# Early slots with the weights' scale alone, three late slots in a row turned by TensorE, and the loop count read after the last scatter

## The chip, the cores and the metric

The kernel runs on one core of a Trainium2 chip. The metric is the device time of one execution in microseconds (us). Three runs of the kernel before gave a median of 835.51 us (831.27 to 840.33).

## The reference

Three stages follow one another; the change touches only the last. B=4, 8 heads, 544 positions of width 64, so 2176 tokens of width 512.

```python
x = attention(q_l, k_l, v_l, q_g, k_g, v_g)      # local window of 32 and 32 global positions; 2176 x 512
h = x @ w_in;  x = (h * sigmoid(h)) @ w_out      # 512 -> 2048 -> 512
logits = x @ w_gate                              # 8 experts
e_idx = np.argmax(logits, axis=1)
gate_w = softmax(logits)[token, e_idx]
eom = 1.0 / (1.0 + np.exp(-(x @ w_output_gate)))
for e in range(8):
    mask = e_idx == e
    h = np.maximum(x[mask] @ w1[e], 0.0)         # w1[e]: 512 x 1024
    ye = h @ w2[e]                               # w2[e]: 1024 x 512
    out[mask] = gate_w[mask, None] * eom[mask, e, None] * ye
```

## The kernel before

**Stages.** Attention takes the first part of the span, the dense layers (L688, L735) follow, and their output is written row by row to `x2d` in DRAM. Each token's expert is found on the way. The expert stage fills the end, from about 530 us on.

**Slots.** The tokens of one expert are gathered into slots of 128 rows. Slots n = 0 to 7 are the early ones, one for each expert; they take tokens of the first 15 of 17 token blocks, so that their rows can be gathered before the last blocks are done. Slots n = 8 to 20 are the late ones (k = n-8 runs from 0 to 12); which expert each one has is known only after the routing. Ten further slots run only if the number of slots asks for them, inside a `tc.If` at the end. Its condition is read from the table `eidx` into a register of every engine (L1560); with these inputs it isn't met.

**Chunks.** The hidden width of 1024 is worked in 4 chunks of 256. A chunk has an h phase (`mm_h`: `hp` = slot's rows by w1, L1317 and L1320, or L1325 in another shape; then relu, a split in two f16 parts `hb` on ACT and DVE, and a DMA transpose of `hb` that SP issues, L1344) and a y phase (`mm_y`: six matmuls `yp`, L1354). The first chunk's `yp` is written out of PSUM by ACT with a factor for each row (L1362), the later chunks' by DVE, which multiplies and adds to what is there (L1364). After the last chunk POOL scatters the slot's rows to `out` (L1366). Two PSUM pools of two buffers each hold `yp`, so TensorE can be up to four slots ahead of ACT.

**The factor.** It is gate_w x eom (`cof`, one for each token) times the scale by which the expert's weights were made f16 (`gi`, one for each expert and chunk). `coefs(c)` makes their product for all slots of chunk c. For the early slots of the first chunk the product `cce` is made ahead of that by `early_coefs()`: 15 small matmuls `pce` (L1143) and some DVE operations.

**Weights.** SP loads the weights of the next chunk piece by piece (`ws`), ACT takes a maximum (L228), and ACT and DVE convert them (L961, L962) into single buffers, in place of the chunk that TensorE has just left.

**Routing.** `last()` makes, from the last two token blocks, the rows of the late slots: TensorE `pm` gives `idg` (which rows to gather), `early_coefs()` follows, then `pt` (L1196) gives `ids` (which rows to scatter to), DVE makes `eidx` and `ohs` (experts of late slots, L1140), and `pcf` (L1217) gives `cof`. `early()` sets the h phase of early slots 2 to 7 and the y phase of early slots 0 to 5 around it. `experts()` (L1244) loads the late slots' expert numbers into TensorE's registers, 13 of them.

**Late rows.** POOL gathers each late slot's rows from `x2d`. Those with k in `TURN` are turned by TensorE (8 transposes `xt` a slot, L1291; ACT or DVE copies the result out of PSUM); the others are turned by a DMA transpose that SP issues (L1260) once the gather has landed.

**Order.** The code is handed to a list scheduler, which sets the order on each engine; `high_priority` and `issue_after` bend it. An instruction waits at the head of its engine's queue, and everything behind it waits too.

Of the kernel before, what the change touches and what calls it, by code (L numbers as in the profile page):

```python
# [26 lines left out]
NE = 8  # L27
# [20 lines left out]
NS = 1  # L48
# [5 lines left out]
TURN = (1, 3, 5, 7, 9, 11)  # L54
# [53 lines left out]
def tile_kernel(ctx: ExitStack, tc, csa, csr, q0, q, qn, qg, k0, k, va, vc, w_in, w_out, wg, w1, w2, out, dbg=None):  # L108
# [876 lines left out]
    cce = const.tile([128, NEARLY], F32, name="cce")  # L985
    bnd = const.tile([128, 1, NE], F32, name="bnd")

    def route(rt, rps):
# [3 lines left out]
        def bc(x, shape):  # L992
            return x.to_broadcast(shape)
# [143 lines left out]
        def early_coefs():  # L1137
            SR = [128, 15, NEARLY]
            for c in range(3):
                DVE.tensor_tensor(Rce[:, :, c], RE, bc(cp[:, c, 0:15], SR), ALU.mult)  # L1140
            pc = rps.tile([128, 3, NEARLY], F32, tag="av", name="pce")
            for i in range(15):
                PE.matmul(pc.rearrange("p c n -> p (c n)"), A[:, i], Rce[:, i].rearrange("p c n -> p (c n)"),  # L1143
                          start=(i == 0), stop=(i == 14))
            v = T([128, 1, NEARLY], "ve")
            DVE.tensor_copy(v[:, 0], pc[:, 2])
            DVE.tensor_tensor(v[:, 0], v[:, 0], pc[:, 1], ALU.add)
            DVE.tensor_tensor(v[:, 0], v[:, 0], pc[:, 0], ALU.add)
            g = T([128, 1, NE], "ge")
            DVE.tensor_tensor(g[:, 0], i12[:, 0:NE], i12[:, NE:2 * NE], ALU.mult)  # L1150
            DVE.tensor_scalar(g, g, 2.0 ** 19, None, ALU.mult)
            DVE.tensor_tensor(cce, v[:, 0], g[:, 0], ALU.mult)

        def last():
# [34 lines left out]
            with tc.issue_after(key_i[0].ins):  # L1189
                early_coefs()  # L1190
# [39 lines left out]
    class Moe:  # L1230
        def __init__(self, slots, ne):
            self.slots, self.ne, self.ns = slots, ne, len(slots)
            self.ev, self.x, self.hT, self.ys, self.hb, self.cc = {}, {}, {}, {}, {}, {}
# [63 lines left out]
        def coefs(self, c):  # L1297
            g = cc_p.tile([128, 1, NE], F32, tag="gi", name="gi")
            DVE.tensor_tensor(g[:, 0], i12[:, 0:NE], i12[:, NE:2 * NE], ALU.mult)
            DVE.tensor_scalar(g, g, 2.0 ** 19, None, ALU.mult)  # L1300
            t = lg.rearrange("p i e -> p (i e)")[:, 0:ND * NE].rearrange("p (n e) -> p n e", e=NE)
# [4 lines left out]
            for k in range(NS):  # L1306
                r = slice(k, ST, NS)
                DVE.tensor_tensor(cc[:, r], cof[:, r], g[:, 0], ALU.mult)
# [37 lines left out]
        def mm_y(self, c, n):  # L1346
# [9 lines left out]
            if c == 0:  # L1356
# [4 lines left out]
                cc = self.cc[0][:, s:s + 1] if self.late else cce[:, n:n + 1]  # L1361
# [9 lines left out]
        def early(self, ny, i0, i1):  # L1371
            with tc.issue_after(i0.ins):
                for n in range(2, self.ne):
                    self.mm_h(n)
# [241 lines left out]
```

## Time and profile before

| | |
|---|---|
| median of three runs | 835.51 us |
| the profiled execution's own time | 835.75 us |
| its span in the trace | 834.0 us |
| PE busy | 759.4 us (91%) |
| PEld busy | 527.4 us (63%) |
| DVE busy | 600.4 us (72%) |
| ACT busy | 517.7 us (62%) |
| POOL busy | 56.8 us (7%) |

PE is TensorE's matmul, PEld its weight load (which runs beside matmuls), DVE is VectorE, ACT is ScalarE, POOL is GpSimd, SP is SyncE. Times in the rows are us from the span's start unless marked ns. An idle time in square brackets stands ahead of the instruction, with the engine, tile and line that ended it. [...]

### The profile page before, as it was taken

The numbers are of one execution on the slowest core, as the hardware profiler recorded it, in microseconds if no ns is written. First come the engines' busy times: TensorE is split into PE (matmuls) and PEld (weight loads), VectorE is DVE, ScalarE is ACT, GpSimd is POOL, SyncE is SP. The second block draws the span as 40 slices with busy tenths as digits, with TensorE's granted clock in tenths as the row PEclk, the third lists the DMA queues.
The fourth block names the chain that finished last, engine by engine and source line by source line (L and its number), as shares of the span: only waits on it lengthen the run. The fifth ranks groups of instructions, "written<-read, shape, count | busy, mean of one in ns | idle before, by whom it ended". The sixth has DMA issues, their size and how long they took to land.

```text
span 834.0 us, 17487 instructions
## 1 busy us (share of the span) xinstructions
PE 759.4 (91%) x6249; PEld 527.4 (63%) x6249; DVE 600.4 (72%) x1653; ACT 517.7 (62%) x1020; POOL 56.8 (7%) x110
## 2 busy tenths in 40 slices
PE   6999949899999989989999989998799798998995
PEld 5998726466776757667766656766566465565552
DVE  4799877767966878747755587749364878878863
ACT  3786667867847758646643895342379666856730
POOL 0000000000000000000000000032300000000144
PEclk9999969999999999999999999999999999999998
DMA  9962552658945475744545865075966746955583
GB/s 321 324 196 88 160 167 102 176 114 195 183 110 74 89 130 119 153 77 77 110 62 103 258 202 153 13 188 131 201 134 189 228 83 171 258 109 165 151 186 104
DMA packets 176235, 126.25 MB, mean 151 GB/s; under 512 B 155149, under 2 KB 156941, under 8 KB 172944
## 3 DMA queue, kind: packets, MB, share of 16 engines
q1 hardware_dynamic: 172784, 115.10, 56.7%
q0 software_dynamic: 3360, 9.97, 4.2%
q8 instruction: 54, 0.88, 0.4%
q14 instruction: 37, 0.30, 0.1%
HBM read 76.93 MB, written 9.96 MB: 104 GB/s over the span
## 4 chain that ended last, share of the span: by engine, by line
PE 41%; DMA 12%; DVE 7%; ACT 5%; issue 3%; SPq 1%; POOLq 0%; ACTq 0%; DVEq 0%
PE h L688 9%; PE x L735 9%; PE yp L1354 9%; PE hp L1325 6%; DMA ws<-in_w_dram 5%; DMA pT<-pb 4%; PE hp L1317 2%; PE av L538 2%; DMA wil<-hb 1%; DVE w1b L962 1%; ACT w1b L961 1%; DMA woh<-yx 1%; PE hp L1320 1%; ACT junk L228 1%; ACT w2b L961 1%
## 5 line engine op out<-in xcount | busy, mean ns | idle before, releaser
L735 PE MATMUL x<-woh,g 128*128 128x512 f16 x544 | 172.3, 379 | 3.5 <-ACT g L718 1.5
L688 PE MATMUL h<-xT,wih 128*128 128x256 f16 (+1 forms) x1152 | 160.4, 271 | 10.1 <-DMA xT<-xb 4.9
L735 PEld LDWEIGHTS <-g 128*128 128x128 f16 x816 | 76.4, 98 | 85.3 <-issue 2.7
L688 PEld LDWEIGHTS <-wih 128*128 128x128 f16 x1152 | 108.1, 100 | 34.2 <-DMA xT<-xb 5.2
L1354 PE MATMUL yp<-w2b,wil 128*128 (+1 forms) x384 | 93.7, 391 | 11.0 <-ACT w2b L961 5.3
L735 PE MATMUL x<-wol,g 128*128 128x512 f16 x272 | 103.1, 379 | 0.0
L688 PE MATMUL h<-xT,wil 128*128 128x256 f16 (+1 forms) x576 | 88.0, 272 | 0.0
L690 ACT ACTIVATE tanh<-h,th 128x512 f32<-128x512 f32 (+1 forms) x72 | 47.2, 658 | 64.0 <-PE h L688 61.4
L470 ACT ACTIVATE e<-e,mx,esc 128x192 f32<-128x192 f32 (+1 forms) x128 | 70.1, 549 | 18.5 <-DVE mx L467 15.5
L1354 PEld LDWEIGHTS <-wil 128*128 128x128 f16 x384 | 38.1, 103 | 51.4 <-DMA wil<-hb 8.4
L707 ACT ACTIVATE g<-tanh,i_out 128x512 f16<-128x512 f32 (+1 forms) x64 | 44.1, 691 | 33.3 <-DVE tanh L703 33.2
L228 ACT ACTIVATE junk<-ws 128x1024 f16<-128x1024 f32 x48 | 50.4, 1052 | 17.4 <-DMA ws<-in_w_dram 17.2
L466 DVE CUSTOM_DVE_ANT_0 e<-s,cs 128x192 f32<-128x192 f32 (+1 forms) x128 | 42.5, 367 | 23.2 <-PE s L455 10.4
L688 PEld LDWEIGHTS <-wil 128*128 128x128 f16 x576 | 54.4, 100 | 7.4 <-issue 0.5
L708 DVE SCALAR_TENSOR_TENSOR g<-tanh,i_out,g 128x512 f16<-128x512 f32 (+1 forms) x64 | 45.6, 713 | 17.0 <-ACT g L707 16.9
L703 DVE SCALAR_TENSOR_TENSOR tanh<-tanh,h 128x512 f32<-128x512 f32 (+1 forms) x64 | 41.4, 649 | 21.3 <-ACT tanh L690 21.0
L962 DVE SCALAR_TENSOR_TENSOR w1b<-ws,s,w1b 128x1024 f16<-128x1024 f32 x32 | 40.4, 1280 | 17.2 <-ACT w1b L961 17.0
L1325 PE MATMUL hp<-w1b,x 128*128 128x256 f16 x384 | 48.7, 279 | 1.2 <-ACT r L1338 1.2
L1325 PEld LDWEIGHTS <-x 128*128 128x128 f16 x384 | 38.6, 102 | 10.7 <-issue 2.1
L523 DVE SCALAR_TENSOR_TENSOR pb<-e,pb 128x384 f16<-128x384 f32 (+1 forms) x48 | 27.6, 586 | 22.9 <-ACT pb L522 22.8
L962 DVE SCALAR_TENSOR_TENSOR w2b<-ws,s,w2b 128x1024 f16<-128x1024 f32 x32 | 40.2, 1280 | 2.6 <-ACT w2b L961 2.6
L1364 DVE SCALAR_TENSOR_TENSOR yx<-yp,cc,yx 128x512 f32<-128x512 f32 x39 | 29.1, 748 | 8.9 <-PE yp L1354 8.8
(361 smaller groups left out, 1447.6 us busy)
## 6 DMA issues: line engine op xcount, KB each, us to landing
ws<-in_w_dram SPq DMA_DIRECT2D x64, 512.0 KB, 4.5
st<-in_w_out_dram SPq DMA_DIRECT2D x8, 1024.0 KB, 5.0
st<-in_w_in_dram SPq DMA_DIRECT2D x6, 1024.0 KB, 12.0
q<-in_q_dram SPq DMA_DIRECT2D x12, 512.0 KB, 4.0
x2d<-x2s SPq DMA_DIRECT2D x17, 256.0 KB, 2.7
st<-in_k_dram SPq DMA_DIRECT2D x3, 1088.0 KB, 7.0
st<-in_qn_dram SPq DMA_DIRECT2D x3, 1024.0 KB, 5.1
st<-in_va_dram SPq DMA_DIRECT2D x3, 1024.0 KB, 6.9
```

What stands on the lines that cost most here:

```text
L228: ACT.activation(junk, x, ACTF.Square, accum_out=m)
L466: DVE.tensor_tensor_reduce(dst[:, hh, 0:wt], ps[:, hh, 0:wt], mask, 1.0, -3e38, ALU.add, ALU.max, mx[:, hh:hh + 1])
L470: ACT.activation(dst[:, hh, 0:wt], dst[:, hh, 0:wt], ACTF.Exp, scale=esc[:, b:b + 1], bias=mx[:, 2 + hh:3 + hh], accum_out=sums[i][:, h:h ...
L688: PE.matmul(ps[:, f], w[:, kk, c], xj[:, l + kk, 0:n], start=(m == 0 and kk == 0), stop=(m == 2 and kk == KD - 1))
L690: pin[0] = ACT.activation(t, ps, ACTF.Tanh, scale=th[:, b:b + 1])
L703: pin[1] = DVE.scalar_tensor_tensor(t, t, 1.0, ps, ALU.add, ALU.mult)
L707: ACT.activation(hi, t, ACTF.Copy, scale=i)
L708: pin[2] = DVE.scalar_tensor_tensor(lo, t, i, hi, ALU.mult, ALU.subtract)
L735: PE.matmul(x2ps[2 * j + c], x[:, f, o], w[:, ff], start=(ff == 0 and m == 0), stop=(ff == KF - 1 and m == 2))
L962: DVE.scalar_tensor_tensor(d[:, 1], t[a], sc_, d[:, 0], ALU.mult, ALU.subtract)
L1325: PE.matmul(ps[:, 0], x[:, xl + kk], self.rows("1", n, l, kk), start=(m == 0 and kk == 0), stop=(m == 2 and kk == KD - 1))
L1354: PE.matmul(ps, h[:, hl + j], self.rows("2", n, l, j), start=(m == 0 and j == 0), stop=(m == 2 and j == KJ - 1))
```

## The change

It has three parts.

1. **Early slots carry only the weights' scale.** `early_coefs()` and `cce` go away. `scales(c)` makes `gi` alone, and `early()` calls it at its start. All early slots are written out with `gi` in every chunk, and after the last chunk ACT multiplies each of the eight by `cof` before its scatter. `coefs(c)` no longer makes products for them.
2. **TURN** goes from k = 1, 3, 5, 7, 9, 11 to k = 0, 1, 2, 4, 6, 8.
3. **The `If`'s value** is read on each engine after the last scatter (`issue_after(moe.end.ins)`) instead of where the scheduler put it.

```diff
--- before.py
+++ after.py
@@ -51,7 +51,7 @@
 ND = NSLOT - ST
 NMAIN = 21
 NEARLY = NE
-TURN = (1, 3, 5, 7, 9, 11)
+TURN = (0, 1, 2, 4, 6, 8)
 ORDER = (*range(14), 16, 14, 15)
 POS = {t: r for r, t in enumerate(ORDER)}
 URG = 2000
@@ -982,7 +982,6 @@
     eidx = const.tile([128, ND + 1], I32, name="eidx")
     ohs = const.tile([128, ND, NE], F32, name="ohs")
     idge = const.tile([128, NEARLY], I32, name="idge")
-    cce = const.tile([128, NEARLY], F32, name="cce")
     bnd = const.tile([128, 1, NE], F32, name="bnd")
 
     def route(rt, rps):
@@ -1133,23 +1132,6 @@
                 DVE.tensor_scalar(n0[:, 1], n0[:, 1], 128.0, None, ALU.max)
                 coef(14, 15)
                 static(0, 15)
-
-        def early_coefs():
-            SR = [128, 15, NEARLY]
-            for c in range(3):
-                DVE.tensor_tensor(Rce[:, :, c], RE, bc(cp[:, c, 0:15], SR), ALU.mult)
-            pc = rps.tile([128, 3, NEARLY], F32, tag="av", name="pce")
-            for i in range(15):
-                PE.matmul(pc.rearrange("p c n -> p (c n)"), A[:, i], Rce[:, i].rearrange("p c n -> p (c n)"),
-                          start=(i == 0), stop=(i == 14))
-            v = T([128, 1, NEARLY], "ve")
-            DVE.tensor_copy(v[:, 0], pc[:, 2])
-            DVE.tensor_tensor(v[:, 0], v[:, 0], pc[:, 1], ALU.add)
-            DVE.tensor_tensor(v[:, 0], v[:, 0], pc[:, 0], ALU.add)
-            g = T([128, 1, NE], "ge")
-            DVE.tensor_tensor(g[:, 0], i12[:, 0:NE], i12[:, NE:2 * NE], ALU.mult)
-            DVE.tensor_scalar(g, g, 2.0 ** 19, None, ALU.mult)
-            DVE.tensor_tensor(cce, v[:, 0], g[:, 0], ALU.mult)
 
         def last():
             with tc.high_priority(URG):
@@ -1187,7 +1169,6 @@
                         pm_i = PE.matmul(pm, A[:, i], Rc[:, i, c], start=(i == 0 and c == 0), stop=(i == NT - 1 and c == 1))
                 key_i[0] = DVE.tensor_scalar(idg, pm, -1.0, 0.0, ALU.add, ALU.max)
             with tc.issue_after(key_i[0].ins):
-                early_coefs()
                 for c in range(2):
                     DVE.tensor_tensor(Rc[:, :, c], R, bc(row[2 + c], SR), ALU.mult)
                 pm = rps.tile([128, NSLOT], F32, tag="av", name="pt")
@@ -1230,7 +1211,7 @@
     class Moe:
         def __init__(self, slots, ne):
             self.slots, self.ne, self.ns = slots, ne, len(slots)
-            self.ev, self.x, self.hT, self.ys, self.hb, self.cc = {}, {}, {}, {}, {}, {}
+            self.ev, self.x, self.hT, self.ys, self.hb, self.cc, self.gi = {}, {}, {}, {}, {}, {}, {}
             self.late, self.xg, self.pair = False, [], [None, None]
             for n, x in enumerate(slots):
                 if x < ST:
@@ -1294,18 +1275,20 @@
             else:
                 DVE.tensor_copy(x, p)
 
-        def coefs(self, c):
-            g = cc_p.tile([128, 1, NE], F32, tag="gi", name="gi")
+        def scales(self, c):
+            g = self.gi[c] = cc_p.tile([128, 1, NE], F32, tag="gi", name="gi")
             DVE.tensor_tensor(g[:, 0], i12[:, 0:NE], i12[:, NE:2 * NE], ALU.mult)
             DVE.tensor_scalar(g, g, 2.0 ** 19, None, ALU.mult)
+
+        def coefs(self, c):
+            if c not in self.gi:
+                self.scales(c)
+            g = self.gi[c]
             t = lg.rearrange("p i e -> p (i e)")[:, 0:ND * NE].rearrange("p (n e) -> p n e", e=NE)
             DVE.tensor_tensor(t, ohs, g.to_broadcast([128, ND, NE]), ALU.mult)
             cc = self.cc[c] = cc_p.tile([128, NSLOT], F32, tag="cc", name="cc")
             DVE.tensor_reduce(cc[:, ST:], t, AX.X, ALU.add)
             DVE.tensor_tensor(cc[:, ST:], cc[:, ST:], cof[:, ST:], ALU.mult)
-            for k in range(NS):
-                r = slice(k, ST, NS)
-                DVE.tensor_tensor(cc[:, r], cof[:, r], g[:, 0], ALU.mult)
 
         def mm_h(self, n):
             x = self.x[n]
@@ -1358,17 +1341,22 @@
                     self.ys[n] = ysv[:, n]
                 else:
                     self.ys[n] = self.room(n - self.ne, 1)
-                cc = self.cc[0][:, s:s + 1] if self.late else cce[:, n:n + 1]
+                cc = self.gi[0][:, 0, n:n + 1] if n < self.ne else self.cc[0][:, s:s + 1]
                 ACT.activation(self.ys[n], ps, ACTF.Copy, scale=cc)
             else:
-                DVE.scalar_tensor_tensor(self.ys[n], ps, self.cc[c][:, s:s + 1], self.ys[n], ALU.mult, ALU.add)
+                cc = self.gi[c][:, 0, n:n + 1] if n < self.ne else self.cc[c][:, s:s + 1]
+                DVE.scalar_tensor_tensor(self.ys[n], ps, cc, self.ys[n], ALU.mult, ALU.add)
+            if c == NCH - 1 and n < self.ne:
+                ACT.activation(self.ys[n], self.ys[n], ACTF.Copy, scale=cof[:, s:s + 1])
             if c == NCH - 1:
                 ins = POOL.indirect_dma_start(out=out[:, :], out_offset=bass.IndirectOffsetOnAxis(ap=ids[:, s:s + 1], axis=0),
                                               in_=self.ys[n], in_offset=None, bounds_check=NTOK - 1, oob_is_err=False)
                 tc.declare_no_dep(ins.ins, group="sc", reason="every row is written once")
                 tc.add_to_no_dep_group("sc", ins.ins)
+                self.end = ins
 
         def early(self, ny, i0, i1):
+            self.scales(0)
             with tc.issue_after(i0.ins):
                 for n in range(2, self.ne):
                     self.mm_h(n)
@@ -1557,7 +1545,9 @@
         ys_p = ctx.enter_context(tc.tile_pool(name="ys", bufs=1))
         moe.ys_p, moe.late = ys_p, True
         moe.rest(P["nye"], wq1)
-    with tc.If(nc.values_load(eidx[0:1, ND:ND + 1], min_val=0, max_val=ND) > NMAIN - ST):
+    with tc.issue_after(moe.end.ins):
+        more = nc.values_load(eidx[0:1, ND:ND + 1], min_val=0, max_val=ND)
+    with tc.If(more > NMAIN - ST):
         with ExitStack():
             moe = Moe(list(range(NMAIN, NSLOT)), 0)
             moe.ys_p, moe.late = ys_p, True
```

The rows below are each engine's program in its order, without times; `xN` stands for N alike in a row. Lines of the kernel after differ from those before: L1196 is L1177 there, L1244 L1225, L1354 L1337, L1217 L1198, L1344 L1327, L1260 L1241, L1258 L1239, L1366 L1352.

TensorE at the routing, before: the end of `pt`, then the load of the experts' numbers, ahead of early slot 2's `yp`.

```order
L1196 LDWEIGHTS A
L1196 MATMUL pt<-wil,A 128x31
L1244 TENSOR_LOAD eidx
L1244 ISA x8
L1354 LDWEIGHTS wil
L1354 MATMUL yp<-w2b,wil 128x512
```

The same place after: slot 2's six `yp` stand between `pt` and the load, and `pcf` right behind it.

```order
L1337 LDWEIGHTS wil
L1337 MATMUL yp<-w2b,wil 128x512
L1225 TENSOR_LOAD eidx
L1225 ISA x18
L1198 LDWEIGHTS A
L1198 MATMUL pcf<-wil,A 128x93
```

The load has moved behind six matmuls `yp`, and 18 register instructions instead of 8 follow it at once; 8 more stand after one slot's `yp` behind `pcf`. From `pm` on, TensorE's order was: 12 `yp`, 15 `pce`, 34 `pt`, load, 6 `yp`, 17 `pcf`, 6 `yp`, `xt` of k = 1 (16 with k = 3), one `hp` of k = 0, 6 `yp`, rest of k = 0, k = 2, 6 `yp`, `xt`, k = 1. It is now: 12 `yp`, 34 `pt`, 6 `yp`, load, 17 `pcf`, 12 `yp`, `xt` of k = 0 and 1, 6 `yp`, 6 `yp` (slot 6, formerly much later), `xt` of k = 2, `hp` of k = 0, `xt` of k = 4, `hp` of k = 1, `xt` of k = 6, `hp` of k = 2, `xt` of k = 8, k = 3, and so on. At the border between the first and the second chunk 24 `yp` now stand in a row.

SP's queue at the same time, before: the transposes of the early slots' `hb` (L1344) and of late rows (L1260, `woh` and `wol` hold them).

```order
L1344 DMA_TRANSPOSE wil<-hb 128x8x128 x3
L1260 DMA_TRANSPOSE woh<-yx 128x8x128
L1344 DMA_TRANSPOSE wil<-hb 128x8x128
L1260 DMA_TRANSPOSE woh<-yx 128x8x128
L1560 TENSOR_LOAD eidx
L1560 ISA x2
L1260 DMA_TRANSPOSE woh<-yx 128x8x128 x2
L1260 DMA_TRANSPOSE wol<-yx 128x8x128 x3
L1344 DMA_TRANSPOSE wil<-hb 128x8x128 x4
```

After:

```order
L1327 DMA_TRANSPOSE wil<-hb 128x8x128 x4
L1549 TENSOR_LOAD eidx
L1549 ISA x2
L1241 DMA_TRANSPOSE woh<-yx 128x8x128 x3
L1241 DMA_TRANSPOSE wol<-yx 128x8x128 x4
L1327 DMA_TRANSPOSE wil<-hb 128x8x128 x4
```

All four `hb` transposes stand ahead now; there are seven row transposes as before, the first of them for k = 3 instead of k = 0. SP's own read of the `If`'s value has no matmul or scatter ahead of it, only these.

POOL's end, before: the scatters of the eight early slots (`wih`), of twelve late slots, the `If` with the ten further slots inside, and one last scatter behind it.

```order
L1366 DMA out_dram<-wih,ids 2176x512 x8
L1366 DMA out_dram<-yx,ids 2176x512 x12
L1560 TENSOR_LOAD eidx
L1560 COMPARE_AND_BRANCH
L1258 DMA yx<-x2d,idg 128x1024 x10
L1366 DMA out_dram<-yx,ids 2176x512 x10
L1560 UNCONDITIONAL_BRANCH
L1560 ISA
L1560 UNCONDITIONAL_BRANCH
L1366 DMA out_dram<-yx,ids 2176x512
```

After:

```order
L1352 DMA out_dram<-wih,ids 2176x512 x8
L1352 DMA out_dram<-yx,ids 2176x512 x13
L1549 TENSOR_LOAD eidx
L1550 COMPARE_AND_BRANCH
L1239 DMA yx<-x2d,idg 128x1024 x10
L1352 DMA out_dram<-yx,ids 2176x512 x10
L1550 UNCONDITIONAL_BRANCH
L1550 ISA
L1550 UNCONDITIONAL_BRANCH
```

The thirteenth late slot's scatter has moved ahead of the read and the branch. On ACT the eight new scalings (`wih` by `cof`) stand in the last chunk among the h phase's work: four in a row ahead of one `hb`, the next three and the last one each ahead of a later `r`.

## Rows read from the trace of the kernel before

**Rows 1.** The page: the chain that ended last, share of the span by engine.
```profile
PE 41%; DMA 12%; DVE 7%; ACT 5%; issue 3%; SPq 1%; POOLq 0%; ACTq 0%; DVEq 0%
```

**Rows 2.** Table by stretch: length, busy us of PE, PEld, DVE, ACT, POOL, clock.
```profile
584.00:588.00 4.00, 3.55 (x43) 2.54 (x43) 1.62 (x7) 1.94 (x3) 3.09 (x4) 1.00 1.20 243
592.00:596.00 4.00, 1.84 (x8) 1.02 (x9) 0.04 (x1) 0.00 (x0) 0.95 (x1) 0.84 1.24 247
596.00:600.00 4.00, 4.00 (x29) 2.48 (x28) 0.69 (x1) 1.71 (x2) 0.00 (x0) 0.73 0.93 249
600.00:616.00 16.00, 16.00 (x132) 12.04 (x130) 9.53 (x24) 7.67 (x19) 0.00 (x0) 1.00 0.91 145
612.00:645.00 33.00, 33.00 (x218) 21.14 (x216) 17.57 (x44) 29.65 (x51) 0.00 (x0) 1.00 0.61 164
711.00:714.00 3.00, 3.00 (x16) 2.14 (x15) 0.95 (x4) 2.33 (x5) 0.00 (x0) 0.50 1.02 363
```

**Rows 3.** PE in order of time: start, us, line, count, [idle before <-releaser].
```profile
578.55 0.53 PE L1143 MATMUL pce<-ohs,A 128*128 128x24 bf16 x15
578.93 1.01 PE L1196 MATMUL pt<-wil,A 128*128 128x31 bf16 x34
582.58 1.47 PE L1354 MATMUL yp<-w2b,wil 128*128 128x512 f16 x6 [2.64 <-ACT wih L1362]
584.49 0.92 PE L1217 MATMUL pcf<-wil,A 128*128 128x93 bf16 x17 [0.45 <-DVE wil L1214]
...
594.15 0.93 PE L1325 MATMUL hp<-w1b,woh 128*128 x5 [3.96 <-DMA woh<-yx]
...
708.58 0.60 PE L1354 MATMUL yp<-w2b,wil 128*128 128x512 f16 x2 [2.66 <-ACT w2b L961]
```

**Rows 4.** The chain that ended last, in order of time: start, us, what.
```profile
584.29 9.73 DMA woh<-yx
...
691.61 4.06 DMA ws<-in_w_dram
...
823.88 4.69 DMA out_dram<-yx,ids
```

**Rows 5.** L1244, the experts' numbers into PE's registers: ns minimum/median/maximum.
```profile
L1244 PEldq FUSED_REGOPS  x13: 146/146/165, 581.3 to 585.3; - x13
...
L1244 PEldq TENSOR_LOAD <-eidx x1: 1319/1319/1319, 579.9 to 579.9; - x1
```

**Rows 6.** DVE in order of time around the routing.
```profile
576.26 0.67 DVE L1140 TENSOR_TENSOR ohs<-ohb,cp 128x120 bf16<-128x120 bf16 x3
...
581.13 0.15 DVE L1152 TENSOR_TENSOR cce<-ve,ge 128x8 f32<-128x8 f32 x1
...
583.72 0.71 DVE L1214 TENSOR_TENSOR wil<-wil,cp 128x527 bf16<-128x527 bf16 x1
```

**Rows 7.** Gathers of L1258 (first and last start), then landing of L1260's transposes.
```profile
L1258 POOL DMA_INDIRECT yx<-x2d,idg x7: 940/946/946, 576.6 to 592.2; - x7
...
DMA to landing us min/median/max: 3.5/8.9/12.7
```

**Rows 8.** The last scatters: POOL and DVE in order of time.
```profile
823.88 0.97 POOL L1366 DMA_INDIRECT out_dram<-yx,ids  x1 [0.33 <-DVE yx L1364]
824.15 0.75 DVE L1364 SCALAR_TENSOR_TENSOR yx<-yp,cc,yx 128x512 f32<-128x512 f32 x1 [0.54 <-PE yp L1354]
829.54 0.97 POOL L1366 DMA_INDIRECT out_dram<-yx,ids  x1 [4.68 <-DMA out_dram<-yx,ids]
```

**Rows 9.** L1366, the scatters from 780 us on: issue to landing.
```profile
DMA to landing us min/median/max: 2.5/3.3/6.0
```

**Rows 10.** L1362, ACT's eviction of a 128x512 slot, 612 to 645 us: ns.
```profile
L1362 ACT ACTIVATE yx<-yp,cc x12: 672/703/763, 623.5 to 641.2; 128x512 f32<-128x512 f32 x12
```

**Rows 11.** DVE, and ACT, in order of time in the last chunk.
```profile
792.02 0.74 DVE L1364 SCALAR_TENSOR_TENSOR wih<-yp,cc,wih 128x512 f32<-128x512 f32 x1
...
793.13 0.42 ACT L1335 ACTIVATE hb<-r 128x256 f16<-128x256 f32 x1 [4.13 <-DVE r L1334]
```

## The prediction

> **What bounds the kernel now.** I read the page's chain first: TensorE has 41% of it, more than all else together [rows 1], so a wait of TensorE is where this change can pay. The stretch table from 584 to 645 us shows where the routing costs it time: 1.84 us busy of 4.00 between 592 and 596, and the granted clock down to 0.84 and 0.73 in two stretches, then 1.00 again [rows 2]. From 612 to 645 TensorE is busy for all of the 33.00 us, with ACT at 29.65 [rows 2]: what it gains ahead of 600 is carried on, as no outside event holds it there. (The weights that it meets later are converted into buffers that it frees itself, so their loads move with it; I count on that.)
>
> TensorE in order of time names three waits: 2.64 us for ACT's eviction of an early slot, 0.45 us for DVE ahead of `pcf`, and 3.96 us for a DMA transpose ahead of slot k = 2's last matmuls [rows 3]. Sum 7.05. The transpose was issued at 584.29 and took 9.73 us [rows 4]. The clock's fall costs 4.00 x (1 - 0.84) = 0.64 and 4.00 x (1 - 0.73) = 1.08, together 1.72 us. So the routing loses 8.77 us.
>
> At the end, the last scatter is issued at 829.54, although the DVE operation that makes its rows runs from 824.15 for 0.75 us [rows 8]. It stands behind the `If`, and POOL waited 4.68 us there for the landing of the scatter before it.
>
> **A: the routing.** Removed: the 15 `pce`, 578.93 - 578.55 = 0.38 us of TensorE [rows 3], and the wait of 2.64, since ACT now needs `gi` alone, which is made long before. The wait does not simply vanish: `pcf` needs DVE's last product, and that is now the next thing that is late. Before, this product ended at 583.72 + 0.71 = 584.43 [rows 6]. Gone from DVE ahead of it are 0.67 us of `ohs` [rows 6] and eight small operations of `early_coefs` and `gi`, each like the 0.15 us of `cce` [rows 6]; they overlap, so between 0 and 1.2, and I take 0.5. `pcf` can start at 584.43 - 0.67 - 0.5 = 583.3. TensorE reaches it at 578.55 + 1.01 (`pt`) + 1.3 (six `yp`; 1.47 with the overlap [rows 3]) = 580.9. It then waits about 2.5 us. The register load must also pass: 1.32 us, and nine pairs of instructions, by the span of the 13 recorded ones (581.3 to 585.3 over 12 steps) 0.33 us at most each [rows 5], together 4.3. Started when `pt` has been handed out, near 579.5, it ends at about 583.8 and adds little; started only after the six `yp` it holds `pcf` to 585.2, a wait of 4.3. Before, its instructions ran while matmuls were still at work (581.3 to 585.3, `yp` from 582.58), so I take 2.5, bounds 2.5 to 4.3.
>
> The clock: the wait of 2.64 left it at 1.00 between 584 and 588, while a wait of 2.66 before 708.58 [rows 3] was followed by 0.50 between 711 and 714 [rows 2]. A lone wait of 2.5 can go either way: 0 or 1.72. I take 1.7.
>
> Row transposes: `TURN` now gives k = 0, 1, 2 to TensorE, and the first slot that a DMA turns is k = 3. Its gather stands one place behind that of k = 2, 1.30 us (the seven gathers shown lie at every second place of 13 from 576.6 to 592.2: 15.6 / 12) [rows 7]. If its transpose takes the same 9.73, it lands at 584.29 + 1.30 + 9.73 = 595.3. TensorE has until then: 583.3 + 0.75 (`pcf`, 0.92 with its overlap [rows 3]) + 24 `yp` (four slots of 1.3, 5.2) + the `xt` of k = 0, 1, 2, 4, 6, 8 (48 with a quarter of `yp`'s columns, so 48 x 1.3 / 6 / 4 = 2.6) + the h phases of k = 0, 1, 2 (as many columns as a `yp` slot, 3.9), in sum 595.8. That just covers it. The transposes landed 3.5 to 12.7 us after issue, 8.9 in the middle [rows 7], so a wait between 0 and the 3.96 of before; I take 0.7. The moved `xt` are the same number of instructions, 48, and their evictions lie beside the `yp`. SP's own read of the `If`'s value stands ahead of the seven transposes, at a time when SP waits for the gather anyway; I cost it at nothing, and at 1.3, as on TensorE [rows 5], if that cover is gone.
>
> A in sum: 8.77 + 0.38 - 2.5 - 1.7 - 0.7 = 4.25 us. Best, without the clock's fall and the DMA wait: 6.65. Worst: 9.15 - 4.3 - 1.72 - 3.96 = -0.8.
>
> [...]
>
> **B: the end.** Before, the last scatter was issued at 829.54; now it stands directly behind its predecessor, which was issued at 823.88 and held POOL for 0.97 us, with 0.33 between [rows 8]. It can issue at 825.2, 4.4 us sooner. The read of the `If`'s value and the branch now follow it; in the old order about 1 us lay between the predecessor's landing (823.88 + 4.69 = 828.57 [rows 4]) and 829.54, and I set that against the gain: 3.4. If the last scatter then takes the 4.69 of its predecessor [rows 4] instead of the 2.5 at the lower end [rows 9], 2.2 more are lost: 1.2. I take 2.8, near the upper bound, since the median landing is 3.3 [rows 9].
>
> **C: eight scalings on ACT**, each 0.70 us by ACT's eviction of the same shape [rows 10], 5.6 us in all. ACT sat idle for 4.13 us before `hb` at 793.13 [rows 11], which takes most of the first four. The fourth must wait for DVE's eviction that ends at 792.02 + 0.74 = 792.76 [rows 11] and ends itself at 793.46, 0.3 after the `hb` behind it could have started. I take -0.3. Without the idle time they would cost 2.8.
>
> **D and E.** `scales(0)` puts two small DVE operations far ahead of the routing, at most 0.15 us each [rows 6]: -0.2. The border between the first and the second chunk now has 24 `yp` in a row; the same work in another order, taken at nothing. If it makes weights late, each late load costs 4.06, as the one at 691.61 [rows 4].
>
> **Sum.** 4.25 + 2.8 - 0.3 - 0.2 = 6.55 us. The profiled execution took 835.75, all but the median of 835.51. 835.75 - 6.55 = 829.2 us.
>
> **The rivals.** R1, the routing runs smoothly: no fall of the clock and no late transpose, 2.4 us more, so 826.8. For it: the wait of 2.64 that cost no clock [rows 2]. Against it: the wait at `pcf` is followed by work that depends on gathers still landing. R2, DMA transposes are late again: the wait of 3.96 comes back at k = 3 instead of 0.7, 832.4. For it: the landing up to 12.7 [rows 7], and three transposes queued behind each other; against it: three slots' work now lies ahead. R3, the clock falls once more: TensorE's stretch with 48 transposes among few matmuls lowers the granted clock again, another 1.72, 830.9; the stretch 600 to 616, in which the last 16 `xt` of before lie, at 1.00 [rows 2] speaks against it. [...] R4, slower: at the border of the chunks the weights come late because 24 `yp` in a row keep the old w2 longer and no h phase hides it. It takes 6.55 of late loads (two of 4.06) to cancel the gain, and 14.9, four of them, to be slower by 1%. Nothing in the stretch 612 to 645, where TensorE is never idle, speaks for four. R5, the move of the `If` does nothing, because the end waits for the landing as before: 829.2 + 2.8 = 832.0.
>
> **How the numbers follow.** My forecast 829.2 has a chance of 0.44; R1 0.27, R2 0.15, R3 0.05, R4 0.05, R5 0.04. About 1%, 8.4 us, is what a measurement of this kernel can tell from no change, so the border lies at 827.2. R1 puts most of its chance below it, and my forecast some, as its terms are uncertain by 2 us: faster 0.38. R4's far end gives slower 0.06, and 0.56 remain within 1%. The range goes from 823.5 (R1, with the full 3.4 at the end and 2 us of the 1% scatter of the runs' median) to 834.5 (R2 with B at 1.2 and some).
>
> **What would show it.** In the changed profile: one wait of 2 to 3 us ahead of `pcf`, released by DVE; no wait for ACT's eviction; 0 to 1 us for a transpose at k = 3; a stretch near 0.75 of the clock between 584 and 600 or none; the last two scatters 1.3 us apart; and TensorE without a gap until the border of the chunks, where it would begin about 4 us earlier. Wrong would be a wait of 4 us or more at k = 3 or at `pcf`, weights later than the work, or a last scatter that lands no sooner.

## The result, and the profile after

The changed kernel took 827.37 us, the kernel before 837.32 us (medians of six runs each; three of before's six are those taken ahead of the prediction). The ratio is 0.989, with an interval of 0.985 to 0.993. In a second comparison it was 827.31 against 838.08 us, ratio 0.985 (0.979 to 0.991). The profiled execution took 825.79 us with a span of 824.0, against 835.75 and 834.0 before. The forecast was 829.2, with a gain of 6.55 us; the gain is about 10.

After `pm` the kernels run the same matmuls, apart from the 15 `pce`. So I cut each profile by counting TensorE's matmuls back from the last one and taking their start times: from the first `pm` to the 1234th before the last (the routing, into the first chunk's late slots), to the 959th (end of the first chunk), to the 534th (the border to the second chunk and beyond), to the 134th, to the 34th (the last chunk's y phase has begun), and to the span's end. Times in us; the kernels are those of the experiments below.

| kernel | first `pm` | routing | to 959 | to 534 | to 134 | to 34 | tail | span |
|---|---|---|---|---|---|---|---|---|
| before | 575.1 | 33.50 | 47.21 | 74.55 | 67.53 | 18.72 | 17.35 | 834.0 |
| before again (e8) | 571.3 | 34.05 | 48.14 | 75.48 | 69.36 | 18.53 | 17.17 | 834.0 |
| If alone (e1) | 579.0 | 31.97 | 48.16 | 75.33 | 69.28 | 18.59 | 14.84 | 837.2 |
| TURN alone (e2) | 574.4 | 29.29 | 47.63 | 74.37 | 67.66 | 18.57 | 16.26 | 828.2 |
| scaling alone (e3) | 575.5 | 30.26 | 49.72 | 73.11 | 66.37 | 17.74 | 16.24 | 828.9 |
| after | 575.9 | 29.28 | 47.69 | 71.72 | 67.71 | 16.89 | 14.85 | 824.0 |
| after again (e5) | 573.2 | 29.33 | 48.79 | 73.09 | 68.87 | 16.89 | 14.81 | 824.9 |
| other order (e4) | 572.3 | 28.71 | 48.00 | 72.75 | 66.99 | 17.53 | 15.97 | 822.3 |
| pcf later (e6) | 575.8 | 25.08 | 47.97 | 72.71 | 68.67 | 16.89 | 14.82 | 821.9 |
| load later (e7) | 573.1 | 28.61 | 47.85 | 72.53 | 68.11 | 17.51 | 14.92 | 822.7 |
| old border (e9) | 570.4 | 38.11 | 49.51 | 74.73 | 67.38 | 18.67 | 16.91 | 835.7 |
| pcf last (e10) | 580.5 | 35.77 | 48.46 | 73.69 | 68.24 | 19.48 | 16.87 | 843.0 |
| pcf later again (e11) | 579.4 | 36.61 | 47.96 | 72.09 | 67.78 | 18.70 | 16.83 | 839.3 |
| pcf last again (e12) | 578.7 | 36.54 | 47.71 | 72.50 | 68.09 | 19.19 | 17.16 | 839.9 |

The first column shows why one time of one run says little: work that the change all but leaves alone ends anywhere from 570 to 580 us. By the two profiles each of before and after, the mean gains are 4.5 us in the routing, -0.6 to the 959th, 2.6 to the 534th, 0.2 to the 134th, 1.7 to the 34th and 2.4 in the tail: 10.8 in all. The routing of e1, in the order of before, took 31.97 us; with it before's mean is 33.2 and the gain there 3.9.

TensorE at the routing, after, in order of time (columns as in [rows 3]):

```profile
579.31 1.02 PE L1177 MATMUL pt<-wil,A 128*128 128x31 bf16 x34
580.17 1.46 PE L1337 MATMUL yp<-w2b,wil 128*128 128x512 f16 x6
584.84 0.98 PE L1198 MATMUL pcf<-wil,A 128*128 128x93 bf16 x17 [3.21 <-DVE wil L1195]
585.61 4.42 PE L1337 MATMUL yp<-w2b,wil 128*128 128x512 f16 x12
```

The three waits of 2.64, 0.45 and 3.96 us [rows 3] are gone; one of 3.21 has come, the only one until 640 us. The stretch table (columns as in [rows 2]) shows the granted clock behind it, as a share of TensorE's full clock (the number after POOL's):

```profile
584.00:588.00 4.00, 3.16 (x23) 1.69 (x24) 0.86 (x5) 0.00 (x0) 2.94 (x4) 0.69 1.09 281
588.00:592.00 4.00, 4.00 (x29) 2.12 (x28) 0.69 (x1) 1.37 (x2) 2.93 (x4) 0.88 0.97 271
592.00:596.00 4.00, 4.00 (x35) 2.54 (x34) 0.92 (x2) 2.56 (x4) 1.80 (x2) 1.00 1.17 268
```

It falls once, at 0.69 and 0.88, and costs 4.00 x 0.31 + 4.00 x 0.12 = 1.72 us, as much as before. The row transposes (L1241), issue to landing:

```profile
DMA to landing us min/median/max: 3.3/6.1/6.6
```

They were 3.5/8.9/12.7 [rows 7], seven of them in either kernel. At the end, POOL:

```profile
816.42 0.97 POOL L1352 DMA_INDIRECT out_dram<-yx,ids  x1 [0.32 <-DVE yx L1348]
817.72 0.97 POOL L1352 DMA_INDIRECT out_dram<-yx,ids  x1 [0.32 <-DVE yx L1348]
```

The last two scatters are 1.30 us apart, where they were 5.66 apart [rows 8]. From the last one's issue to the end of the span it is now 6.3 us (824.0 - 817.72), before 4.5 (834.0 - 829.54). The first experiment shows where this goes.

### The profile page after: what moved, and what is told of

The parts are those of the page before. It is cut to its first block, busy times and chain, and to the rows that moved or that the text cites. A ratio compares the mean times of both kernels' runs of the same rounds, so it can differ in the third digit from the quotient of the medians.

```text
span 824.0 us, 17450 instructions
## 1 busy us (share of the span) xinstructions
PE 759.2 (92%) x6234; PEld 526.6 (64%) x6234; DVE 599.9 (73%) x1642; ACT 521.0 (63%) x1026; POOL 56.8 (7%) x110
## 4 chain that ended last, share of the span: by engine, by line
PE 62%; DMA 13%; DVE 10%; ACT 7%; issue 5%; SPq 1%; POOL 0%; POOLq 0%; ACTq 0%; DVEq 0%
PE h L688 16%; PE x L735 14%; PE yp L1337 7%; PE hp L1308 5%; DMA ws<-in_w_dram 5%; DMA pT<-pb 4%; PE hp L1300 3%; PE av L538 3%; PE s L481 3%; ACT w1b L961 2%; PE av L505 2%; PE av L504 2%; DVE w1b L962 1%; ACT junk L228 1%; DMA xT<-xb 1%
## 5 line engine op out<-in xcount | busy, mean ns | idle before, releaser
L1337 PE MATMUL yp<-w2b,wil 128*128 (+1 forms) x384 | 93.6, 392 | 4.2 <-ACT w2b L961 1.9
L1337 PEld LDWEIGHTS <-wil 128*128 128x128 f16 x384 | 38.1, 102 | 44.8 <-issue 6.9
L521 POOL MEMSET pb<- 128x256 f16 (+1 forms) x48 | 12.4, 259 | 327.3 <-DMA pT<-pb 135.8
```

Source lines behind the costliest of these rows:

```text
L1337: PE.matmul(ps, h[:, hl + j], self.rows("2", n, l, j), start=(m == 0 and j == 0), stop=(m == 2 and j == KJ - 1))
```

## The experiments

**One part alone.** First the `If`:

```diff
 # kernel before
+                self.end = ins
 ...
-    with tc.If(nc.values_load(eidx[0:1, ND:ND + 1], min_val=0, max_val=ND) > NMAIN - ST):
+    with tc.issue_after(moe.end.ins):
+        more = nc.values_load(eidx[0:1, ND:ND + 1], min_val=0, max_val=ND)
+    with tc.If(more > NMAIN - ST):
```

> Kernel before with only the read of the If's value moved behind the last scatter. TensorE's order up to the last matmul is that of before. My theory (three separate gains: routing 3.8 us, middle of the expert stage 3.7 us, end 2.5 us in the two profiles): 2.5 us faster, all of it between TensorE's last matmul and the span's end (9.9 us before, 7.4 after the whole change), ratio 0.997. Rival (the end waits for the landing of the scatters anyway, and the shorter tail of the changed kernel comes from its other parts): the tail stays at 9 to 10 us, ratio 1.000.

The tail was 14.84 us, as after the whole change, and 2.4 less than the mean of before's two profiles. The last scatter was issued 1.07 us after TensorE's last matmul, 5.43 in before; yet the span did not gain 4.4 us by it. First before, then this kernel: the landing of the last scatter, and POOL's closing instruction:

```profile
DMA to landing us min/median/max: 2.7/2.7/2.7
L1612 POOLq DRAIN  x3: 40/113/3825, 829.3 to 833.7; - x3
```

```profile
DMA to landing us min/median/max: 3.0/3.0/3.0
L1615 POOLq DRAIN  x3: 40/107/1780, 834.6 to 836.9; - x3
```

The transfer itself took nearly the same time. But in before the long `DRAIN` ran beside it and ended 0.9 us after the landing (832.23). Now it starts only when the `If` is through, 0.7 us after the landing (833.86), and ends 2.5 us after it: 1.6 us of the gain go there. The ratio, 1.000 (0.996 to 1.003), can't show so little and is at the edge of what I expected. Its routing has before's order, yet it took 31.97 us and the waits for rows came to this:

```profile
602.63 0.62 PE L1291 MATMUL xt<-id,yx 128*128 128x128 f16 x8 [0.34 <-DMA yx<-x2d,idg]
...
607.22 3.44 PE L1325 MATMUL hp<-w1b,woh 128*128 x24 [0.94 <-DMA woh<-yx]
```

So the 3.96 us [rows 3] are not a fixed cost of that order, nor is before's routing time; the second profile of before (e8) had 1.56 us for the transpose and 0.42 and 1.54 for gathers.

TURN alone:

```diff
-TURN = (1, 3, 5, 7, 9, 11)
+TURN = (0, 1, 2, 4, 6, 8)
```

> Kernel before with only the new TURN. My theory (the late DMA transpose is what TURN takes away): the wait of 3.96 us ahead of slot k = 2 falls below 1 us, the waits of 2.64 and 0.45 ahead of it stay, and without the long wait the clock's fall of 1.72 us at 592 to 600 goes too; TensorE reaches the late slots in steady work 4 to 5.7 us earlier, order of the later chunks and the end as before, ratio about 0.994. Rival (the row transposes are late wherever they stand, since gathers and transposes share the DMA engines): a wait of 3 us or more moves to k = 3 or 5, ratio 1.000.

831.41 us, ratio 0.994 (0.990 to 0.998). The routing was 29.29 us, all of what the whole change reaches. Every wait for rows was gone. In place of the waits of 2.64 and 0.45 stood one of 3.33:

```profile
582.55 2.72 PE L1354 MATMUL yp<-w2b,wil 128*128 128x512 f16 x6 [3.33 <-DVE cf L1080]
585.07 1.33 PE L1217 MATMUL pcf<-wil,A 128*128 128x93 bf16 x17
```

The clock fell behind that wait (0.58 from 582 to 586), so the part of the expectation that it would stay up failed.

The scaling alone (the diff of the change without TURN and `If`):

> Kernel before with only the early slots' new scaling (no early_coefs, eight scalings on ACT in the last chunk). My theory: in the routing it removes the waits of 2.64 and 0.45 us and 0.38 us of pce, and gets one wait of about 3.2 us ahead of pcf and the clock's fall of 1.72 us behind it, while the late transpose of slot k = 0 or 2 stays: within 1.5 us of before there. It also changes the order of the later chunks; if that order is what gave the changed kernel its 3.7 us in the middle, this kernel gains 2 to 4 us there: ratio 0.995 to 0.999. Rival (the scaling is the whole gain, TURN none): the routing is 3.5 us shorter, ratio 0.991. Second rival (the middle differs by chance from one execution to the next): no gain in the middle.

827.8 us, ratio 0.990 (0.985 to 0.995). The routing was 30.26 us, 3.2 to 3.8 shorter than in the two profiles of before (1.7 shorter than in e1): with slots 2 to 5 no longer waiting for the factor, `yp` and `xt` stand ahead of slot k = 0, and the transposes landed in time. So the expectation that they would stay late was wrong. The first rival's numbers came (3.5 us, 0.991), but its reason, that TURN brings nothing, does not stand: alone it brings as much. **In the routing each of the two parts takes the same waits away; together they bring hardly more than one of them.** To the 534th it took 73.11 us, 1.4 to 2.4 less than before, without TURN.

**The order of the later chunks.** The scaling moves no work there, except for small DVE operations and the eight scalings; yet the scheduler gives other orders. To see what another order does, one unused product stays in:

```diff
 # changed kernel, in coefs: an unused 128x8 product for each chunk
+            for k in range(NS):
+                r = slice(k, ST, NS)
+                DVE.tensor_tensor(cc[:, r], cof[:, r], g[:, 0], ALU.mult)
```

> The changed kernel with one unused 128x8 product a chunk left in coefs (what before needed for the early slots; its result is not read). It costs under 0.2 us of DVE a chunk, but the scheduler then puts the matmuls of the later chunks in another order, 8 to 24 matmuls further along at some places; routing and end are those of the changed kernel. My theory (the gain of 3.7 us between 655 and 817 us is one of order at the borders of the chunks): routing and tail as in the changed kernel within 0.5 us, the middle 2 to 5 us longer, ratio to before about 0.993. Rival (the middle gain comes from the removed products or from the matmuls of the routing being earlier, not from order): every stage within 0.7 us of the changed kernel, ratio 0.989.

827.77 us, ratio 0.991 (0.987 to 0.995). To the 534th 72.75 us, inside the 71.7 to 73.1 of the changed kernel: this third order is as good as the second, so the miss here is mine. It doesn't tell whether order matters at all. Its tail was 16.0 us, 1.1 more than after and not within 0.5 as expected, and POOL shows why:

```profile
799.25 0.98 POOL L1355 DMA_INDIRECT out_dram<-wih,ids  x1 [8.80 <-ACT wih L1353]
...
815.86 0.97 POOL L1355 DMA_INDIRECT out_dram<-yx,ids  x1 [0.30 <-issue]
```

In this order ACT's scaling of the eighth early slot came late. The thirteen late scatters queue up behind it, 1.28 us apart without a pause, and the last is issued 2.08 us after TensorE's last matmul (1.07 in the profile after). What tells about order is a kernel with before's order at this border and the rest of the change:

```diff
 # changed kernel: the register load behind pcf; the later chunks then get before's order
-                    PE.matmul(pc.rearrange("p c n -> p (c n)"), A[:, i], Rc[:, i].rearrange("p c n -> p (c n)"),
+                    pcf_i = PE.matmul(pc.rearrange("p c n -> p (c n)"), A[:, i], Rc[:, i].rearrange("p c n -> p (c n)"),
 ...
-            self.experts()
+            with tc.issue_after(self.pcf.ins) if ne else ExitStack():
+                self.experts()
 ...
```

> The changed kernel with the register load behind pcf and the transposes free to move ahead of it. By this TensorE's order from the end of the first chunk to the end of the third chunk's h phase is, matmul for matmul, that of before, with all that the change does otherwise (scaling, TURN, the If). It separates order from content at the border of the first and the second full chunk: the stretch from the 959th to the 634th matmul before the last took 56.6 to 57.1 us in four profiles with before's order and 52.3 to 54.3 in six with the new scaling. My theory (the order of matmuls there is the cause): 56.3 to 57.3 us, with the wait of about 2.66 us ahead of the first yp with the new weights and the granted clock near 0.5 behind it. Rival (the removed products and the new factors free DVE or ACT there, whatever the order): 52 to 54.5 us.

From the 959th to the 634th it took 57.81 us, a little above what I expected for order as the cause and far from the rival's 52 to 54.5; to the 534th 74.73, inside the 74.4 to 75.5 of the four profiles with before's order. The wait was there too; the clock behind it fell less than expected, to 0.82 and 0.61. First the kernel after, then this one, TensorE at the border:

```profile
701.28 5.27 PE L1308 MATMUL hp<-w1b,x 128*128 128x256 f16 x45
706.39 1.46 PE L1337 MATMUL yp<-w2b,wil 128*128 128x512 f16 x6
708.38 0.61 PE L1337 MATMUL yp<-w2b,wil 128*128 128x512 f16 x2 [0.53 <-DMA wil<-hb]
```

```profile
707.25 1.47 PE L1308 MATMUL hp<-w1b,x 128*128 128x256 f16 x12 [1.03 <-ACT r L1321]
711.40 0.61 PE L1337 MATMUL yp<-w2b,wil 128*128 128x512 f16 x2 [2.68 <-ACT w2b L961]
...
714.16 3.84 PE L1308 MATMUL hp<-w1b,x 128*128 128x256 f16 x24
```

In the old order the first `yp` that needs the new w2 stands ahead of two slots of h work (24 `hp`), and TensorE waits 2.68 us for ACT's conversion with this work behind it; in before it was 2.66 [rows 3]. In the new order 45 `hp` run first, while ACT converts. All five profiles with the old order took 74.4 to 75.5 us to the 534th, the nine others 71.7 to 73.7; e10, from the same comparison as e9, took 73.69. The time of e9, 841.69 us against 843.22 for before, ratio 0.999 (0.996 to 1.002), says nothing about the border: its routing had a stall of 7 us, of which more below. The clock behind the wait is no part of it for certain: it was at 0.50 in before [rows 2], but 1.00 from 700 to 720 in before again, which took as long. What made the last chunk's border 1.7 us shorter (18.5 to 18.7 us in the four profiles with before's scaling, 16.9 to 17.7 in the first six with the new one) was not tried alone. In those four TensorE waited 1.48 to 1.67 us there for a DMA transpose of `hb`; of the six, e7 waited 0.45 us for one and the others not at all. That this comes from the order too is argued, not shown.

**What holds `pcf`.** The profile after names DVE, whose last product is this row:

```profile
583.40 0.71 DVE L1195 TENSOR_TENSOR wil<-wil,cp 128x527 bf16<-128x527 bf16 x1
```

It ends at 584.11, but `pcf` starts at 584.84. The register load at that place (times in ns, first and last start in us):

```profile
L1225 PEldq FUSED_REGOPS  x13: 146/146/165, 582.2 to 585.9; - x13
L1225 PEldq SEQ_ASSERT  x13: 18/18/28, 582.4 to 586.1; - x13
L1225 PEldq TENSOR_LOAD <-eidx x1: 2227/2227/2227, 579.9 to 579.9; - x1
```

The load took 2.23 us (1.32 in before [rows 5]); nine of the pairs, about 0.29 us apart, stand ahead of `pcf` and end at 584.78. So I moved the load behind `pcf` and one slot's `yp`, and the first transposes `xt` with it:

```diff
-            for j in range(2 * KD):
-                PE.transpose(p[:, j], t[:, 128 * j:128 * j + 128], id16)
+            with tc.issue_after(self.pcf.ins):
+                for j in range(2 * KD):
+                    PE.transpose(p[:, j], t[:, 128 * j:128 * j + 128], id16)
 ...
-            self.experts()
+            with tc.issue_after(self.pcf.ins) if ne else ExitStack():
+                self.experts()
 ...
```

> The changed kernel with the load of the experts' numbers into TensorE's registers behind pcf and one early slot's yp; nothing else moves but the first xt, by one slot's yp. In the changed kernel DVE's last product ends at 584.11, the register instructions ahead of pcf end at 584.78 and pcf starts at 584.84, though the profile names DVE. My theory (the register load holds pcf, and held early slot 2's yp in before too): pcf starts within 0.15 us of DVE's end, the wait is about 2.5 us instead of 3.2. Rival (DVE holds it): pcf 0.7 us after DVE's end as before, wait 3.2 us. Either way the clock falls behind it, and the time is that of the changed kernel within what a measurement tells, ratio 0.988.

DVE, and then TensorE:

```profile
580.68 0.71 DVE L1195 TENSOR_TENSOR wil<-wil,cp 128x527 bf16<-128x527 bf16 x1
```

```profile
581.45 0.91 PE L1198 MATMUL pcf<-wil,A 128*128 128x93 bf16 x17 [2.54 <-DVE wil L1195]
```

DVE ends at 581.39 and `pcf` starts 0.06 later, after 2.54 us. The register load had held it. In before, too, slot 2's `yp` started at 582.58 [rows 3], 0.06 after the last of four register pairs (582.52), while ACT's eviction, which the profile names, had ended at 582.07. And with TURN alone that `yp` started at 582.55, 0.06 after the fourth pair (582.49), behind a load of 2.02 us. The time, 830.86 us, ratio 0.990 (0.983 to 0.996), can't tell 0.7 us.

**A version that fills the wait.** `pcf` behind the y phase of early slots 3 and 4:

```diff
+            def fin():
                 pc = rps.tile([128, 3, NSLOT], F32, tag="av", name="pcf")
 ...
                 for n in range(ny):
                     self.mm_y(0, n)
+                    if n == 4:
+                        fin()
```

> The changed kernel with pcf's 17 matmuls placed behind the y phase of early slots 3 and 4, with the register load ahead of them; the order of TensorE from 600 us on and all other work as in the changed kernel. My theory (TensorE's 3.2 us ahead of pcf and the clock's fall of 1.72 us behind it are both bought by the place of pcf): the wait falls below 0.7 us, the granted clock stays at 1.00, TensorE reaches the late slots' steady work 4 to 4.9 us earlier, and the kernel is 4 to 5 us faster than the changed one, ratio to before about 0.984. Rival (what is won there is lost to the row transposes, which are then late): a wait of 3 us or more at k = 3 or later, ratio as the changed kernel's 0.989.

```profile
584.78 0.92 PE L1200 MATMUL pcf<-wil,A 128*128 128x93 bf16 x17 [0.62 <-DVE wil L1195]
```

823.2 us, ratio 0.979 (0.972 to 0.986), beside 827.31 for the changed kernel in the same comparison. The routing took 25.08 us, 4.2 less than after, and the clock stayed at 1.00. All of it came as expected in this profile. The times alone would not tell: the interval of the changed kernel there, 0.979 to 0.991, overlaps this one.

> Kernel before once more, for a second profile. If the late transpose of slot k = 2 and the waits in the middle are fixed parts of this order, the wait for the transpose is again 3 to 5 us and the stretch from the 1234th matmul before the last to the 34th is again 208 us within 1. If they are chance, the wait is anything from 0 to 5 us and the stretch 208 to 212 us.

One run: 835.81 us. The matmuls from the 1234th to the 34th took 211.5 us instead of 208.0, and the transpose's wait was 1.56: chance, by the expectation's own terms. The second profile of the changed kernel (e5) says the same. I had expected it to be 2.5 to 5 us shorter than before's 208.0 in this stretch, as the first was with 204.0; it took 207.6, so that failed. The stretch as a whole varies by 3.5 us in either kernel. What tells them apart is the stage to the 534th, the one to the 34th and the tail, in which all profiles of either lie on their own side.

With `pcf` one slot later still (`n == 5`):

> The changed kernel with pcf behind the y phase of early slots 3, 4 and 5, so one slot later than in the run that had it behind 3 and 4, and with four of the register instructions' pairs behind that slot's yp. There pcf still waited 0.62 us and started 0.06 us after the last register instruction ahead of it, 0.56 us after DVE. My theory (the register load is what is left): no wait over 0.1 us at pcf, the routing (from pm to the 1234th matmul before the last) 24.4 to 24.8 us instead of 25.1; the kernel as fast as that one within what a measurement tells, ratio to before 0.979 to 0.984. Rival (a later pcf makes the first late slots wait, for cof or for their rows): a new wait of 1 us or more between pcf and the first late slots' yp, ratio 0.985 or more.

838.43 us, ratio 0.993 (0.990 to 0.996), with a stall of 9.55 us in the routing. Neither theory had it. Both versions were run once more side by side:

> The changed kernel with pcf behind early slots 3 and 4, once more, beside the next one on the same chip. If its gain is its own: routing (from pm to the 1234th matmul before the last) 24.8 to 25.5 us, as the 25.1 of its first profile, no stall of more than 1 us there, ratio to before 0.977 to 0.985. If a stall like that of the kernel with pcf behind slot 5 can come to any order of this stretch: a wait of 5 us or more that ends with nothing that the profile names as late, ratio 0.988 or more.

834.41 us, ratio 0.990 (0.986 to 0.994): the second reading.

> The kernel with pcf behind slots 3, 4 and 5, once more. Its first profile had a stall of 9.55 us ahead of slot 5's yp: DVE and ACT took up pt's and slot 3's results only at 596.5, though TensorE's records have these matmuls at 585 to 589. If the stall belongs to this order: again 8 to 11 us at that place, routing 34 to 37 us, ratio 0.990 to 0.996. If it was chance: routing 24.4 to 25 us as first expected, ratio within 0.004 of the kernel beside it.

839.5 us, ratio 0.994 (0.991 to 0.997), with a stall of 8.68 us at the same place and a routing of 36.54. Now the version with `pcf` behind slots 3 and 4 (e11) had the stall as well; DVE and TensorE of it:

```profile
584.94 0.17 DVE L1079 TENSOR_TENSOR cf<-cf,cp 128x2 f32<-128x2 f32 x1
595.34 0.19 DVE L1180 TENSOR_SCALAR oh<-pt 128x31 f32<-128x31 f32 x1 [10.23 <-remote]
```

```profile
584.12 0.99 PE L1177 MATMUL pt<-wil,A 128*128 128x31 bf16 x33
584.96 2.75 PE L1339 MATMUL yp<-w2b,wil 128*128 128x512 f16 x12
598.01 1.49 PE L1200 MATMUL pcf<-wil,A 128*128 128x93 bf16 x17 [10.30 <-DVE wil L1195]
```

TensorE's records have `pt` done at 585.1, and DVE and ACT take up its results and slot 3's only at 595.3 and 595.4. All four profiles of the last two comparisons (e9 to e12) have such a stall at this place (7.0, 9.6, 10.3 and 8.7 us of TensorE); none of the ten others has it. They also have tails of 16.8 to 17.2 us in spite of the moved `If`, and these come from a second, shorter stall of the same kind at the late slots' scatters; e11:

```profile
824.39 2.73 DVE L1350 SCALAR_TENSOR_TENSOR yx<-yp,cc,yx 128x512 f32<-128x512 f32 x4 [2.68 <-PE yp L1339]
```

TensorE's records show its matmuls there without a gap; DVE waits (2.2 to 2.7 us in the four), then takes four slots in a row, and the scatters queue up on POOL. In the stage to the 34th, where the early slots' scatters run, TensorE stands still for 1.0 to 2.1 us in all (up to 0.5 us in the six profiles with the new scaling above). Both stalls lie where POOL's gathers or scatters run; from the 1234th to the 134th matmul, where they hardly do, the four take what the others take. And the landings of POOL's DMAs are on record only in part there: none of its 42 gathers and scatters has a landing time in these four traces, 20 to 42 have one in each of the ten others. So the stall goes together with something about POOL's DMAs; whether it comes from them isn't shown. In those two comparisons the kernel before took 843.2 and 843.8 us, 5 to 6 more than in the others, so it may have had the stall too, but no profile of it was taken there. Neither the order of `pcf` nor the chip alone is the cause: e6 is the kernel of e11 and had no stall, and e1 to e4 ran on the chip of e11 and e12. **What the stall is stays open, and with it whether the version with `pcf` later beats the changed kernel always**: it did by 4 us where they stood side by side; where the stall came, the changed kernel wasn't run.

## Why the prediction was right, and where its terms were off

The time lies inside the range, 1.8 us below the forecast, and the sign was right. That it came so near is in part luck: the forecast started from 835.75 us, but over six runs before came to 837.32, so the gain was 9.95 us and not 6.55. What is missing is about the size of E below. (The range's lower end does not come out of the terms given for it: 826.8 - 0.6 - 2 is 824.2, not 823.5; nothing hangs on it.) By the terms:

- **A, the routing: 4.25 forecast, 4.2 between the two first profiles (33.50 - 29.28), 4.5 by the means of two.** The size was right, its make-up only in part, and the sum by luck: two errors of 0.7 cancel, 8.77 + 0.38 - 3.21 - 1.72 - 0 = 4.22. The wait ahead of `pcf` came, with the clock's fall of 1.72 behind it as taken. But it was 3.21 and 3.22 us instead of 2.5: the step that said the register load "adds little" failed. I had let the load end at 583.8; it took 0.9 us longer than the one row showed and held `pcf` until 584.8. The same step had charged before's 2.64 us to ACT because the profile does, and had read the pairs as running beside matmuls; but they began at 581.3 [rows 5], while TensorE stood still until 582.58 [rows 3]. The row transposes, priced at 0.7, cost nothing in the first profile (the first landed 4.4 us after its issue, not 9.73) and 1.28 in the second, where in turn no clock fell.
- **TURN and the scaling were added up**, as if the waits that each takes away were its own. They were not: TURN alone left a routing of 29.29 us, the scaling alone 30.26, both together 29.3.
- **B, the end: 2.8 forecast, 2.5 measured**, and 2.4 with the `If` alone. The issue moved as worked out, by 4.4. What was set against it was of the right size but the wrong kind: the landing took 0.3 us more, and 1.6 went to the closing `DRAIN`, which no longer runs beside it.
- **C, eight scalings on ACT: -0.3 forecast.** The fourth one stood ahead of `hb` as foreseen:

```profile
783.26 1.94 ACT L1350 ACTIVATE wih<-wih,cof 128x512 f32<-128x512 f32 x3
786.95 0.72 ACT L1350 ACTIVATE wih<-wih,cof 128x512 f32<-128x512 f32 x1 [1.75 <-DVE wih L1348]
787.58 0.40 ACT L1318 ACTIVATE hb<-r 128x256 f16<-128x256 f32 x1
```

  No wait of TensorE follows from it (to the 134th 67.7 and 68.9 us, before 67.5 and 69.4). In another order it can cost: in e4 a late scaling held the scatters, for 1.1 us of tail. **D** (-0.2) is below what the first `pm`'s spread of 10 us can show.
- **E, the order at the chunks' borders: nothing forecast, about 4 us measured** (2.6 to the 534th, 1.7 to the 34th). This is the term that failed. The rows had the wait of 2.66 ahead of a `yp` with new weights [rows 3] and the chain had that conversion in it; I used them only for the clock and for a rival with a loss. That a new order could put work ahead of that wait was a gain to be bounded, 0 to 2.66 at each border, and at one of them it is 2.2 us by the means of the five and the nine profiles. That it is the order is shown for this border by e9; for the last chunk's 1.7 us it is not.
- **The rivals.** R1 gives 826.8, near the measured time, but for reasons that did not hold together: the fall of the clock was there in one profile and the transpose's wait in the other. R2's 3.96 at k = 3 came in no profile. R3's second fall did not come: the clock was at 1.00 from 589 to 600, where the 48 transposes ran; that transposes lower it is not shown. R4 went the other way. R5 is refuted by the tail of e1.

## What to carry to other kernels

Where a scheduler sets the order, an edit can change the time far from where it was made, so don't price the new order there at nothing: look for every wait of TensorE behind which ready work is queued, and give the new order a bound on both sides. Two edits that take away the same wait don't add up, so price each with the other in place. And when a wait has a named releaser that ended well before the wait did, look at the engine's own queue: here it was the load of registers.

## What the runs showed of the hardware that was not expected

A load of 13 numbers into TensorE's registers took 1.32 to 2.23 us for the load itself and about 0.29 us for each pair of instructions after it, in TensorE's own queue, and TensorE stood still for it once its queued matmuls had run out: with the load moved behind `pcf`, `pcf` started 0.06 us after DVE's last product instead of 0.73. The transposing DMAs of the late rows, all of one shape, landed 4.4 to 12.7 us after their issue in the profiles before and after where gathers were still under way, and 3.3 and 3.5 us after it where the last gather had landed. POOL's last scatter, issued 4.4 us sooner, gave back only 2.4 us, because POOL's closing `DRAIN`, which had run beside the last transfer, then took 1.8 us behind it. And a stall of 7 to 10 us, in which other engines see TensorE's results late although its records show them done, came in four profiles, in all of them while POOL's gathers ran, and is not explained.
